# Gate and value halves of a pair's accumulator, and a new order for the first part, in a fused attention and MLP kernel

## The chip, the cores and the metric

The kernel runs on one core of one Trainium2 chip. The metric is the time of one execution on the device, in microseconds (us). Engines are called by their short names in the profile: PE is TensorE (PEld its weight loads), DVE VectorE, ACT ScalarE, POOL GpSimd, and SP the queue that issues most DMAs.

## The reference

The input is a gated linear attention over 4 batches, 8 heads, 768 steps and head size 48, followed by two MLPs over the 3072 tokens.

```
S = 0                                     # complex state, 48 x 48, per batch and head
for t in range(768):
    S = (a_re_n + i a_im_n)[t] * S + k[t] v[t]^T      # a normalised to |a| <= 0.999
    y[t] = q[t] @ S_re
x   = y as 3072 tokens x 384
xn  = x / sqrt(mean(x*x) + 1e-6) * rms_g
x2  = (silu(xn @ w_gate) * (xn @ w_val)) @ w_out      # w_gate, w_val: 384 x 1536
h   = x2 @ w_in                                       # 384 x 2048
out = (h * clip(h + 3, 0, 6) / 6) @ w_out2
```

All inputs arrive in 32 bit floats or, for the weights, as 64 bit words that the kernel turns into 32 bit floats itself. Each large product is made of three matmuls with 32 bit operands split into a high and a low part (`mm3`, lines 735 to 737).

## The kernel before

The time axis is cut into seven units (32 steps twice over at the ends, 64 in between; `UNITS`). A unit goes through these steps, each a small function that issues a few instructions:

- The recurrence of the decay (`steps_norm`, `steps_scan`): 16 or 32 steps of a multiplication (L442) and an addition that reads it (L446) on VectorE, then the scaled keys and queries `X2` and `P`, which also go to memory (L499) and come back as `K` (L536).
- The attention products (`steps_G`): transposes to `psT` (L597), which ScalarE copies to `XTt` (L603); the scores `psS` (L650); the sums `psU` of K and V (L667, L668), from which VectorE makes the new state `Sst` (L638); the outputs `psY` (L678, L687), which ScalarE and GpSimd normalise into `Yt` (L695 to L703); and the transposes to `psX` (L712), split into the halves `xh` and `xl` (L717, L719).
- The first MLP's gate and value products (`steps_M`), for 256 tokens at a time. 12 column blocks j are taken in pairs. One pair has one accumulator tile `pm` in PSUM, 128 partitions of 1024 floats, with two tiles in flight. It holds four quarters of 256: gate and value of the even and of the odd j. Each quarter takes 9 matmuls (three k, three of `mm3`), a tile 36. Then ScalarE applies the Silu to the two gate quarters into `sg` (L756), VectorE multiplies by the two value quarters (L758), and the result goes to memory (L760). There are 12 such passes and 72 tiles.
- In between, weights are loaded and split (L301 to L328) for the first MLP, and then for the rest (`decode`).

All of this, up to about 640 us, is the first part. What sets its order is a long string, `ORDER`: each two characters are the number of a step in the list `steps`, and each time that a number comes up the step issues its next piece. The order of instructions on each engine follows this string, and an engine executes its own in order; semaphores that the framework places keep data right between engines. Behind it follow the second product of the first MLP (`po`, with `uu` read back from memory) and the second MLP (`ph`, `po`), whose order comes from `run` and is not touched.

What the change touches is the tile `pm` in `steps_M` (lines 743 to 767) and the string `ORDER`.

Of the kernel before, what the change touches and what calls it, by code (L numbers as in the profile page):

```python
# [30 lines left out]

DIGITS = "0123456789abcdefghijklmnopqrstuvwxyzABCDEFGHIJKLMNOPQRSTUVWXYZ+-"
ORDER = (
    "000F00010R0R1f0R020R0R0R0R0R020G0R0S0S030S03040S0506080S070b0S0S0b0c0c0S0d0S0H0d120e0T0e0K0T0a0f0T0f0g0T0g0h0h0T090I0i0T0i0j0k0k0T0L0T0J0l0l0m0j0m0n0n0T0o0o0p0U"
    "0p0j0u0q0q0v0r0U0r0v0s0U0t0U0w0t0U0x0U0t0y0z0U1f0U0A170U0A0V11170B0D150V0C1g0V15181h0V0V0V0V0E0V0V11130W0W1h110W181i0W140Q0W110W2r1i0W0W1j0W161k0X2t161a2u1l111b"
    "1n0X1m1z1a2v1z192z1A191A0X1B2s2x2z1B1e1b3b1C2F2y2K0X1C2z1e1D2z1o1d2w1d1D0X1c2A0X2A1E1c2K0OkH2A1E1p2A1F1F0X0X2C1G2B1G2C1H0M1H2D2H0N2K1I1p0X2D1I1q1J1q2G0Y1J0Y1K2D"
    "1r1K1s1L0Y2D2H1L2E2L0Y1v1M2L2L1t2L2M1M2G1N2H1y1N2J0Y2P0Y1u1O2I2P1O2K1Q1Q2N2P1R0Y1R1P2N2N0Y1P1S2N0Y1S0P0Z2O2I2Q1T2I2Q1T2Q1U0Z1U4D1V4J1w0Z1P1V4Q271W4W284E4X1x4F1W"
    "4K280Z4L4P4Y4R2S4S4G4M1X4T4Z0Z0Z4+4U1X4V0Z504-1Z291Y4H2g0Z4N1Z501+2Z511+gj2Z1-570Z581-1Y0Y20202b212+4O0Z4I2+1Y5253210+2V220+220+230+4m2d2V230+242e592425502e5a4P"
    "262f0+2W2a26540+265e2h2c5k2i3b2R5f2j5b0+555l0+2k2W565m2X4l5n5d2R5c0-2X5o5g2-5p2k2R2l2n2m2-5d2R2Y5h5r4p5x4t0-2o2Y305s5t4p3c5i5u2R5y0-304p2T324t0-0-5d2R2R5j374n0-"
    "5v2U32314p5q4o3d4r5q3d4q375q5E5z4t0-314t5A3e5w5F394v4s395B4u0-4v0-344v3410364v10363535383e5C3f103a5D4w3a4w4w105G4w333g103h5H3j104x1010383i3v4P5I5J5K4z104z4z5R3v"  # L40
    "5L5M5R3w334B5N4z3w5O5D5P4A3x5S5T7z5R3x3y3y5S5S5Q4y3z4C3z6a5Q5Z5+3A5U5U3k636g3A6b5-6c6d606e3l3B5U616h3B3C3C5Q5D643D3D5U3E65623l6i6j663E4y3F6k676f6m3F3m693G686l69"
    "3G6m5V5V6A3H693m3n6n3H6B6t6o6u6G3o5V3I3p6m6H6v6w6C3I4C3J3J3K3K3q6p3r6x0W3L6q5V3M6y0R6r3M5W6I3N6D3N6J3O6E3O6s6z6K3P6z6L6z3P6F6M3Q5X3L6M5X7b6+3L3s3Q6-743R3R7b3S43"
    "6N3S703T6T6U3T752q6V6O3V445X6W763V7b773t715X785Y7c446P3W6Q45793U3W726X6M7a3X6Z7c6R6S736Y4c7c3X7a6Z3u3Y3Y7m7l7l3Z9c3Z9d3+8-9i463+3-9e3U9j953-906Z40963U409k479f41"
    "497e42977m9192424a7z4e8J9l9893999m9a424a9g944b7h7i9b7a4f9n4d9h8K9b4g7h4g7d4h7i7n7d9o4j9o7d9p7n9v9b9w9x9q9y7d9r9z489C7d9A4i4k7A9s9I9D7j9E7B7f8R7d9B9F7d9t9G8N7B8R"
    "9J9u7j9o9H8N9B9K9L9M7k7k7C7o8N8L7o7p7C7q9P8N7g9Q9O7D9N8O7p9V7E7q7F8R7v7r7r8P7v7u8M7x9R9O7Ga07H9Wa1a28T7I9B9S8T7x9Ta67J8Ra39X9Y7u7T8S8T7y7T8T7s7U7U7J8U8U7K7Va47V"
    "7W9-7W7X8Ua77X8U8Va5a89U7s8Q7Y7Y7K9Z7Z7y9+8X7Z8X7+7+9-7-8X7t7L7t7-807wa97w9O808Xaaab8Z8Yad7MaeafbX81adae81ad82ae9-8Wayacac7N82alaraEagasatam7P8383au84agazan84ag"
    "aFaGaxacaoaHav85apaA85aBawag8WaqaI86aJ7O86aC88aDah8+ah88aKaxaY87aK87b289ah898a8a8bahaLaM7SaZaR8baN8c8ca+8daOaP878+8db38e7Q8r8eaSaQaT8saxb4aUa-aVb00+8f8f8gaW8hb5"
    "b18hai0Tb68s8i8gb7aXbzajajaK8t8ibzbzaXbJb8b88j8jbKbmd6b9ajbfbabb8kbn8A8k8l8lbg7Rbobsaj8ub8bJ8gbh8m8x8y8makbAbpbc8nbiaXbj8n8obdbtbkbA8obubXd5bv8p8q8y8zblbqbebAbr"
    "bybB8vbBblbwbxbydNdTdOdPdQ8qbydnbl8qbKbB8B8C8Ddt8EdUdV8E8wdodp8FdudvbLbBdqdrdsdR8HdwbL8Gddd9dz8IdxdZdydWdzbBdSdXdYbGdAbYbCbGdGbDbZdHdZbBdBdIdddCd+bEd9d9bFbBbHbZ"
    "d7b+dDd9dzd-e4e0dae5e1dJdEbHb+e2dMbFdZdKdLe3b-e6dFbIc0c3dMbMc1bIdbdfddbMbOc4bObNead8c2bPe7eoc5e8dddfcfbPc5e9epdebUbUeacfebeqdfcgbNdfeubVcgchc6bVbSchbSdgcidgcicj"  # L50
    "cjeackbWckdgbQbWdMerevdgc6ehcleiclcmc7cmcnecejcnewc8dhdjcobQdjcecobRcpbTdjbRc9cpcbexcqescccqdjdceydkeddlcrekcreecsbTen0ScsctcteCeAcueBelefemeBeCcaegeBcueteCezeE"
    "cweAeDdmencwdieWeJcxcvePcxcyf0eKeEencyeLeQczeReXeMeSczcveVcAf1eTeYeEdieAcAeUeNeOcveZeEcBe+cPeFcdcBeFeVeFf2cCcCf3cDfkflfmcDcEf4eFdmf5eGcFe-eHcQeHf6cFfqcQfrfsftcG"
    "cGfnf6eHeHf7cHeIfdeVcHfecIfof8cIf6cEfufpf+fwcRcJcJffcKcKfXcLcEcLf9fvcScYfjcMfwfgcMfhfafbficTfcfxfjcNfXfycOfzcOfDfKfAfEfBcVfYfQcWfXfFcOc+fGc-fRfZd0fYd0fjfLd1fHfC"
    "fJfIfMfwfZfYcWfNgjfShufJfZfTfUhYg6fVi20-cXcUfOfZfWfPg6d3hZ0Ui3h+cZi4gkfWhth-hBi5fZfZimi6fJgli7d4hBi0ini1i8isioi8d2itf-iuivipfWhLgliqgmhxfZhxg4gmgng4g3g3hvg5g7iw"
    "hRhxg7irhxhSg5g0ixgohyg1hzg2gpiyg1g2grg8hBgsiygqhMhBhNiyhThDi9g8ifhOhUiahwhXhPgag9hDgthDg9gthCgagbgDgDgdhQgEhDhVgbgEigihgdibgugFgFhWiihXgegGgugcgcgvgGgHhEhEgfhA"
    "gei8gggHicgwidijgIizikiFiGieiAgIgJiHgxgJilgfhEhEhFiBgygKgKgggLgLhHilgzhHgMiliLiMiSgMiChHgNgNiTiZgOhXhJgOgPiUiVgPiIgQiJgQiDiZgRgRhHhIiEi+gSgSgUgUiNiZiOiKiWgVgViX"
    "gWiPj0i+iQiRiLghi+iYgWgii-gXiYgXjijjjoj0gYgTjkgYgZjljmj5gZiLjng+jbj6g+jpj0g-gTjcj0ghgijd10g-hGh1j7hGjqh1h2jrjsjej8gTh0iYjfh2j9jghbjtgBjhh3h3jah4j1gCj1hKjujhjujI"
    "jujvh4h5jwjOjxjPh5h6jygAj1h6jJh7jQh0jRh7h0jKhcjSh8j1jzh8h9jBjLhc0XhdjCjMjTjAjDjEhfhKjNj2kjhhjFhahiklhajHjhjGkHj3hmjUjUjHj3k6hakcjVjWhikdk7klhnhgklj-kehokjkljUk8"
    "k9j3kihkk0kflkhjkghollklkjhlk1j3hphrloj4kkkkk2jXklkakhkIjHjYkkklkbk3k5jZhek4j+kikulokrkmk5lPlokulChslDlIkrhqlsk5lEkJlQlFlRkJkKlskKlGlVlWlSlJkilKknkpktlmkplLlolX"
    "lTlYkLlZlHlUlOlMlNlOktl+l-kvlslnkqkokvlql-kMkskPkqlpkNkwksmdlrmjlum0lsm1mkmem6mfkwmlm7mglukOkxkykQlukxltkykSkRkAkzlulvkSkTkAkTkUlvkUkVkVkBkzkDmhmilvkWkWkXkXmmmn"  # L60
    "kYkYlvq6kDkZkZm8k-mom2m3m4m9l-mpmak-lwlyl0l0kBlOk+kFl1kCkFmpmclylyl1mDk+mQm5mQ2pmbmcmQmJmEl2l2mKmFlyl3lAmql3lzl4mwl4l5mxk+mRmRmRmTmLkCl5mrmGmHmMmsmpmNl6mymzmImO"
    "l6mAmPkEmPkGmSl7mtkGn9ocl9l8nanbnfl8mumBnglanhmPmvlanclbmCockEndl8mCmTldnemcmYnimTnjlelxnklxn2nlmZm+nlmToclflfn3lgn4nmnsntmClim-nulcmUlBq4mUocq4nnnonvn5npmUnwq5"
    "n6q4ocnln7n0nymUljmVq4nqocnrn1lhlBq5q4nxocogq5q7oimWq4nymWoiq4n8ohogojmWn8mWq5ojoenzq6nZq6odq6nAq5n+oqq8n-nyq5oaq6oaq6nFo3o4o0q5q7o5o1o6oamXoro7o2ohq6nGq8q7o9ou"
    "n8q9obobo8nBnCnHnIosoboko9ouq7ouolnJq7nMolnNnDofnEqanLq7q7nSounTnUq8nKnOovnPoko9nVnWoyowotnLonq8oyomoyoyq8q8nQoAonq8oVqaoAomoWo-nYqbnLp0p1oxp2oXnRqanXoAozooopoA"
    "oBoBnYoIq9p5oOoPoJq9q9oooKnYq9qaqaoYoQoZo+qcoLq9qaqdoRoMoBp3opq9p4oUoSoBp5oNoCoToEqaqboEqboEqcoDoHqbpjoUp6pppcqcp7qcpqp8qcoEqbpkqcpdpeqboFprplp9pfpsqbpgpaqdoGqd"
    "p5phqdqcqdptpupZpmqeoHpvqdpnpbpZqeoUqepZoDpipop+pvp+pipWpvqfpXpJpwp+p+pxpWpypPpCqeqepDpzpEp-pKpXpQpLq0q0pipApBq0qdpMqfpFq0pGpNpRqfqfpXpHpSpVqfpTpOpWq1pUqeq3q2pY"
    "qfpVq3qfq2pIpI0VpIpZqepVq2q3"
)
# [1051 lines left out]
```

## Time and profile before

| | us |
|---|---|
| Median of 3 runs | 1206.21 (1202.79 to 1368.59) |
| Profiled execution | 1208.78 |
| Its span, from the first to the last instruction | 1207.0 |
| TensorE busy | 1089.3 (90%) |
| VectorE busy | 779.7 (65%) |
| ScalarE busy | 544.1 (45%) |
| Mean granted clock of TensorE | 0.974 |

The busy time of an engine is the time in which it had at least one instruction; matmuls overlap, so their durations add up to more. Idle time of an engine is put down to what ended it: the line and tile behind an arrow is the work whose end let the instruction go. The granted clock is a share of 2.4 GHz.

### The profile page before, as it was taken

To read this page: it belongs to the slowest core of one execution; us is meant where nothing else is said; L and a number is where in the kernel's file an instruction comes from. 1 tells how busy PE (TensorE), PEld (TensorE's weight loads), DVE (VectorE), ACT (ScalarE), POOL (GpSimd) and SP (SyncE) were. 2 spreads that over 40 slices of the span, in tenths; PEclk is the share of its full clock that TensorE was granted. 3 is DMA by queue.
4 is the path that set the end of the run, shared out by engine and by line. 5 is a ranking of instruction groups with operands and counts; after the bars stand their busy time and mean duration, and the time that the engine had idled before them with its cause. 6 is when DMAs were issued, how large, how long until landed. Compare 5 with 4: busy or idle time off the path is not lost.

```text
span 1207.0 us, 24591 instructions
## 1 busy us (share of the span) xinstructions
PE 1089.3 (90%) x10264; PEld 944.4 (78%) x10264; DVE 779.7 (65%) x1501; ACT 544.1 (45%) x930; POOL 72.8 (6%) x99
## 2 busy tenths in 40 slices
...
GB/s 252 143 173 140 130 46 237 132 88 231 102 107 184 78 98 206 112 118 153 144 177 302 283 191 101 52 44 1 64 68 1 62 70 1 57 31 1 27 1 29
DMA packets 81433, 133.71 MB, mean 111 GB/s; under 512 B 32225, under 2 KB 50786, under 8 KB 80674
## 3 DMA queue, kind: packets, MB, share of 16 engines
...
q10 hardware_dynamic: 656, 0.11, 0.1%
HBM read 89.77 MB, written 34.60 MB: 103 GB/s over the span
## 4 chain that ended last, share of the span: by engine, by line
PE 42%; DVE 5%; DMA 4%; issue 1%; ACT 1%; DVEq 0%; SPq 0%; ACTq 0%
PE po L736 8%; PE po L737 8%; PE po L735 8%; PE ph L735 5%; PE ph L736 5%; PE ph L737 5%; DMA rawc<-in_wgv_dram 3%; PE pm L735 1%; PE pm L736 1%; PE pm L737 1%; DVE wmin L311 1%; DVE words L303 1%; DMA ok_dr<-okc 1%; DVE ul L906 1%; DVE words L301 0%
## 5 line engine op out<-in xcount | busy, mean ns | idle before, releaser
L735 PE MATMUL pm<-xh,wg 128*128 128x256 f32 x864 | 262.3, 304 | 26.6 <-ACT sg L756 20.6
L736 PE MATMUL pm<-xl,wg 128*128 128x256 f32 x864 | 250.3, 290 | 1.5 <-DVE xl L719 1.5
L737 PE MATMUL pm<-xh,wg 128*128 128x256 f32 x864 | 249.6, 289 | 0.0
L735 PEld LDWEIGHTS pm<-xh,wg 128*128 128x128 f32 x864 | 170.4, 197 | 38.1 <-ACT sg L756 25.6
L736 PEld LDWEIGHTS pm<-xl,wg 128*128 128x128 f32 x864 | 170.8, 198 | 1.8 <-DVE xl L719 1.7
L737 PEld LDWEIGHTS pm<-xh,wg 128*128 128x128 f32 x864 | 170.6, 197 | 0.0
L950 DVE SCALAR_TENSOR_TENSOR r<-r,ph 128x512 f32<-128x512 f32 x96 | 65.9, 686 | 104.0 <-ACT r L949 103.8
L952 DVE TENSOR_TENSOR gl<-r,gh 128x512 fp32r<-128x512 f32 x96 | 68.0, 709 | 94.8 <-ACT gh L951 94.5
L736 PE MATMUL po<-gl,w_h 128*128 128x512 f32 x288 | 114.3, 397 | 4.0 <-DVE gl L952 4.0
L949 ACT ACTIVATE r<-ph,biasz 128x512 f32<-128x512 f32 x96 | 65.9, 687 | 112.7 <-PE ph L737 112.5
L737 PE MATMUL po<-gh,w_l 128*128 128x512 f32 x288 | 114.3, 397 | 0.0
L735 PE MATMUL ph<-x2b,wi_h 128*128 128x512 f32 x288 | 113.8, 396 | 0.4 <-DVE r L950 0.4
L736 PE MATMUL ph<-x2b,wi_h 128*128 128x512 f32 x288 | 113.6, 394 | 0.1
L737 PE MATMUL ph<-x2b,wi_l 128*128 128x512 f32 x288 | 113.6, 395 | 0.0
L951 ACT ACTIVATE gh<-r 128x512 fp32r<-128x512 f32 x96 | 60.7, 633 | 114.1 <-PE po L737 87.1
L735 PE MATMUL po<-gh,w_h 128*128 128x512 f32 x288 | 107.1, 396 | 0.0
L906 DVE TENSOR_TENSOR ul<-uu,uh 128x512 fp32r<-128x512 f32 x72 | 52.1, 725 | 71.6 <-ACT uh L905 71.6
L736 PE MATMUL po<-ul,wo 128*128 128x512 f32 x216 | 85.9, 398 | 3.2 <-DVE ul L906 3.1
L905 ACT ACTIVATE uh<-uu 128x512 fp32r<-128x512 f32 x72 | 45.4, 630 | 94.8 <-PE po L737 77.7
L756 ACT ACTIVATE sg<-pm 128x512 f32<-128x512 f32 x72 | 42.4, 597 | 99.1 <-PE pm L737 78.7
L737 PE MATMUL po<-uh,wo 128*128 128x512 f32 x216 | 84.9, 393 | 0.0
L758 DVE TENSOR_TENSOR sg<-sg,pm 128x512 f32<-128x512 f32 x72 | 48.7, 683 | 47.3 <-ACT sg L756 15.6
(130 smaller groups left out, 1999.4 us busy)
## 6 DMA issues: line engine op xcount, KB each, us to landing
...
```

The lines of the kernel that those rows point to most:

```text
L303: nc.vector.scalar_tensor_tensor(out=A, in0=lo, scalar=29, in1=A, op0=ALU.logical_shift_right, op1=ALU.bitwise_or)
L735: nc.tensor.matmul(ps, lhsT=wh, rhs=xh, start=first, stop=False)
L736: nc.tensor.matmul(ps, lhsT=wh, rhs=xl, start=False, stop=False)
L737: nc.tensor.matmul(ps, lhsT=wl, rhs=xh, start=False, stop=last)
L756: nc.scalar.activation(sg, pm[:, :, 0], AF.Silu)
L758: tt(out=sg, in0=sg, in1=pm[:, :, 1], op=ALU.mult)
L905: nc.scalar.activation(uh, uu, AF.Copy)
L906: (nc.gpsimd if n < 0 else nc.vector).tensor_tensor(out=ul, in0=uu, in1=uh.bitcast(F32), op=ALU.subtract)
L949: nc.scalar.activation(r, ph, AF.Relu, bias=biasz[:, 2:3], scale=sixth)
L950: stt(out=r, in0=r, scalar=1.0, in1=ph, op0=ALU.min, op1=ALU.mult)
L951: nc.scalar.activation(gh, r, AF.Copy)
L952: tt(out=gl, in0=r, in1=gh.bitcast(F32), op=ALU.subtract)
```

## The change

The tile `pm` is indexed by half first and by j second, so that the two gate quarters are one piece of 512 floats, and the two value quarters another. In the list of steps the gemms of a pair now stand half by half: both gates, then both values. The string `ORDER` is another one throughout; of its 38 lines the first is shown.

```diff
-    "000F00010R0R1f0R020R0R0R0R0R020G0R0S0S030S03040S0506080S070b0S0S0b0c0c0S0d0S0H0d120e0T0e0K0T0a0f0T0f0g0T0g0h0h0T090I0i0T0i0j0k0k0T0L0T0J0l0l0m0j0m0n0n0T0o0o0p0U"
+    "0F0R0R0000010G0R0R020R0R0R0R0J0R020S0S03030S0405060L080S070S0H0I0b0b0c0c0c090d0d0N0S0e0e0f0f0g0g0S0S0h0h0S0i0i0T0k0K0k0l0j0j0l0T0j0m0T0m0a1f0u0n0n0T0o0T0o0p0T0T0p"
...
-            mm3(hold[j // 2][:, j % 2, w], wh[:, k, w], wl[:, k, w], xh[:, k], xl[:, k], k == 0, k == KT - 1)
+            mm3(hold[j // 2][:, w, j % 2], wh[:, k, w], wl[:, k, w], xh[:, k], xl[:, k], k == 0, k == KT - 1)
...
-            nc.scalar.activation(sg, pm[:, :, 0], AF.Silu)
+            nc.scalar.activation(sg, pm[:, 0], AF.Silu)
             yield
-            tt(out=sg, in0=sg, in1=pm[:, :, 1], op=ALU.mult)
+            tt(out=sg, in0=sg, in1=pm[:, 1], op=ALU.mult)
...
-        for j in range(J1):
+        for i in range(J1 // 2):
             for w in range(2):
-                for k in range(KT):
-                    out.append((("gemm", h, j, w, k), lambda j=j, w=w, k=k: gemm(j, w, k)))
-            if j % 2:
-                out.append((("silu", h, j), lambda j=j: silu(j)))
+                for j in (2 * i, 2 * i + 1):
+                    for k in range(KT):
+                        out.append((("gemm", h, j, w, k), lambda j=j, w=w, k=k: gemm(j, w, k)))
+            out.append((("silu", h, 2 * i + 1), lambda i=i: silu(2 * i + 1)))
```

The number of instructions of each kind and shape is the same on every engine. Three places of the order:

On PE, in the fourth unit's first pass of `steps_M`, the tile `pm_4675`, the 34th of the 72, before (a name's number tells buffers apart; `[waits ...]` names the engine whose semaphore the instruction waits for, where it does):

```order
L735 MATMUL pm_4675<-xh_4345,wg_313 128x256
L736 MATMUL pm_4675<-xl_4346,wg_313 128x256
L737 MATMUL pm_4675<-xh_4345,wg_313 128x256
L735 MATMUL pm_4586<-xh_4345,wg_763 128x256 [waits Activation_49]
L736 MATMUL pm_4586<-xl_4346,wg_763 128x256
L737 MATMUL pm_4586<-xh_4345,wg_763 128x256
L735 MATMUL pm_4675<-xh_4345,wg_342 128x256 [waits Activation_49]
L736 MATMUL pm_4675<-xl_4346,wg_342 128x256
L737 MATMUL pm_4675<-xh_4345,wg_342 128x256
L735 MATMUL pm_4675<-xh_4345,wg_342 128x256
```

The same tile of the change, there `pm_4607`:

```order
L735 MATMUL pm_4607<-xh_4308,wg_396 128x256
L736 MATMUL pm_4607<-xl_4309,wg_396 128x256
L737 MATMUL pm_4607<-xh_4308,wg_396 128x256
L735 MATMUL pm_4607<-xh_4308,wg_396 128x256 [waits Activation_49]
L736 MATMUL pm_4607<-xl_4309,wg_396 128x256
L737 MATMUL pm_4607<-xh_4308,wg_396 128x256
L735 MATMUL pm_4765<-xh_4308,wg_924 128x256 [waits DVE_49]
```

Before, the mark stands behind the tile's 18th matmul, since its Silu was issued there; in the change it stands behind the 33rd, with three left. The first matmul into a further tile waits for VectorE's multiplication out of an older one, in both.

On DVE, at the start of the first unit's recurrence, before:

```order
L442 TENSOR_TENSOR m4_158<-LAt_110,P_100 128x192
L328 SCALAR_TENSOR_TENSOR wg_151<-wdA_108,gcol_66,wg_151 128x256
L446 TENSOR_TENSOR P_100<-m4_158 128x2x48
L442 TENSOR_TENSOR m4_163<-LAt_110,P_100 128x192
L446 TENSOR_TENSOR P_100<-m4_163 128x2x48
L442 TENSOR_TENSOR m4_167<-LAt_110,P_100 128x192
L328 SCALAR_TENSOR_TENSOR wg_151<-wdA_108,gcol_66,wg_151 128x256
L446 TENSOR_TENSOR P_100<-m4_167 128x2x48
```

and in the change:

```order
L442 TENSOR_TENSOR m4_164<-LAt_110,P_100 128x192
L446 TENSOR_TENSOR P_100<-m4_164 128x2x48
L442 TENSOR_TENSOR m4_167<-LAt_110,P_100 128x192
L446 TENSOR_TENSOR P_100<-m4_167 128x2x48
L442 TENSOR_TENSOR m4_172<-LAt_110,P_100 128x192
L446 TENSOR_TENSOR P_100<-m4_172 128x2x48
```

The pieces of the weight split that stood between a multiplication and its addition come later here, so the pairs stand back to back.

On SP, the loads of the start, before (V is the values of the first unit, S its keys and queries, `wraw` raw weights):

```order
L316 DMA wraw_170<-in_wgv_dram 128x1536
L526 DMA V_173<-in_v0_dram 64x1536
L316 DMA wraw_179<-in_wgv_dram 128x1536
L431 DMA S00_182<-in_s_all_dram 128x768
L431 DMA S01_197<-in_s_all_dram 128x768
L316 DMA wraw_199<-in_wgv_dram 128x1536
L316 DMA wraw_210<-in_wgv_dram 128x1536
L316 DMA wraw_213<-in_wgv_dram 128x1536
L345 DMA LAt_110<-in_a_all_dram 128x3072
```

and in the change:

```order
L316 DMA wraw_162<-in_wgv_dram 128x1536
L431 DMA S01_170<-in_s_all_dram 128x768
L316 DMA wraw_175<-in_wgv_dram 128x1536
L316 DMA wraw_199<-in_wgv_dram 128x1536
L431 DMA S00_214<-in_s_all_dram 128x768
L316 DMA wraw_257<-in_wgv_dram 128x1536
L345 DMA LAt_110<-in_a_all_dram 128x3072
L526 DMA V_260<-in_v0_dram 64x1536
L316 DMA wraw_326<-in_wgv_dram 128x1536
```

The load of V moves behind the second load of `LAt`, and more weights are fetched ahead of it.

## Rows read from the trace of the kernel before

**Rows 1.** The page's totals: busy us (share of the span) and instructions by engine.
```profile
PE 1089.3 (90%) x10264; PEld 944.4 (78%) x10264; DVE 779.7 (65%) x1501; ACT 544.1 (45%) x930; POOL 72.8 (6%) x99
```

**Rows 2.** Stretches: length, busy us (instructions) PE PEld DVE ACT POOL, clock, DMA, GB/s.
```profile
40.00:280.00 240.00, 204.58 (x3093) 188.40 (x3092) 217.50 (x459) 149.97 (x267) 11.50 (x24) 0.96 0.47 143
280.00:636.00 356.00, 326.75 (x4789) 309.42 (x4790) 270.20 (x551) 179.90 (x318) 25.29 (x40) 0.95 0.49 138
636.00:1207.00 571.00, 556.13 (x2374) 445.18 (x2372) 258.46 (x416) 196.88 (x317) 26.55 (x25) 0.99 0.24 72
```

**Rows 3.** Waits of PE, 280 to 636 us: us in total, times, longest.
```profile
PE pm L735 <- ACT sg L756: 15.8, 16, 3.7
PE psU L667 <- DMA K<-k_dr: 4.7, 5, 3.0
PE psY L678 <- ACT Yt L703: 2.5, 1, 2.5
...
PE pm L735 <- DVE sg L758: 1.0, 3, 0.3
```

**Rows 4.** Waits of PE, 40 to 280 us.
```profile
PE pm L735 <- ACT sg L756: 4.8, 4, 2.2
```

**Rows 5.** Timeline of PE: start, us, instruction [idle before <- what ended it].
```profile
360.81 0.58 PE L735 MATMUL pm<-xh,wg 128*128 128x256 f32 x1 [3.68 <-ACT sg L756]
...
371.74 0.28 PE L737 MATMUL pm<-xh,wg 128*128 128x256 f32 x1
372.71 0.38 PE L735 MATMUL pm<-xh,wg 128*128 128x256 f32 x1 [0.69 <-ACT sg L756]
```

**Rows 6.** Timeline of ACT around the same two places.
```profile
358.86 1.28 ACT L756 ACT_TABLE_LOAD   x1
360.16 0.60 ACT L756 ACTIVATE sg<-pm 128x512 f32<-128x512 f32 x1
...
372.06 0.60 ACT L756 ACTIVATE sg<-pm 128x512 f32<-128x512 f32 x1 [1.45 <-PE pm L737]
```

**Rows 7.** Groups of instructions, whole span: count | busy us, mean ns | idle before.
```profile
L949 ACT ACTIVATE r<-ph,biasz 128x512 f32<-128x512 f32 x96 | 65.9, 687 | 112.7 <-PE ph L737 112.5
...
L758 DVE TENSOR_TENSOR sg<-sg,pm 128x512 f32<-128x512 f32 x72 | 48.7, 683 | 47.3 <-ACT sg L756 15.6 <-PE pm L737 13.5 <-issue 6.8
...
L756 ACT ACTIVATE sg<-pm 128x512 f32<-128x512 f32 x72 | 42.4, 597 | 99.1 <-PE pm L737 78.7 <-DMA u_dr<-sg 15.3 <-DVE m L442 4.9
```

**Rows 8.** Half-clock stretches: one, sums over three and over six; last, full clock.
```profile
359.40:366.20 6.80, 5.39 (x25) 5.39 (x26) 1.94 (x4) 4.57 (x8) 0.00 (x0) 0.50 0.02 8
...
sum 13.40, PE 11.99 PEld 11.03 DVE 5.93 ACT 6.13 POOL 0.00; mean PE 4.00 PEld 3.68 DVE 1.98 ACT 2.04 POOL 0.00
...
sum 33.50, PE 31.09 PEld 30.06 DVE 21.29 ACT 13.97 POOL 0.79; mean PE 5.18 PEld 5.01 DVE 3.55 ACT 2.33 POOL 0.13
...
367.00:387.00 20.00, 17.92 (x150) 16.66 (x148) 13.31 (x34) 9.76 (x17) 0.00 (x0) 1.00 0.89 263
```

**Rows 9.** Timeline of DVE in the first unit's recurrence.
```profile
22.20 0.36 DVE L442 TENSOR_TENSOR m<-LAt,P 128x192 f32<-128x192 f32 x1
22.47 0.55 DVE L301 TENSOR_SCALAR wdA<-wraw 128x768 int32<-128x768 int32 x1
...
25.40 0.36 DVE L442 TENSOR_TENSOR m<-LAt,P 128x192 f32<-128x192 f32 x1
25.79 0.26 DVE L446 TENSOR_TENSOR P<-m 128x96 f32<-128x96 f32 x1
```

**Rows 10.** Timeline of SP: DMAs issued at the start.
```profile
34.87 0.33 SPq L345 DMA_DIRECT2D LAt<-in_a_all_dram  x1
...
48.32 1.80 SPq L536 DMA_DIRECT2D K<-k_dr  x4
```

**Rows 11.** Waits of DVE, 40 to 280 us.
```profile
DVE sg L758 <- ACT sg L756: 2.4, 2, 1.3
DVE sg L758 <- PE pm L737: 2.3, 2, 2.0
```

More of the change, by code (lines that the diff above doesn't have):

```diff
@@ L67 @@
-    "qfpVq3qfq2pIpI0VpIpZqepVq2q3"
+    "0F0R0R0000010G0R0R020R0R0R0R0J0R020S0S03030S0405060L080S070S0H0I0b0b0c0c090d0d0N0S0e0e0f0f0g0g0S0S0h0h0S0i0i0T0k0K0k0l0j0j0l0T0j0m0T0m0a1f0u0n0n0T0o0T0o0p0T0T0p"
+    "0T0q0v0q0v0r0T0r0s0U110w0t0U0t0x0y0M1f120t17170U0z150A0U150U0U0A0B0U0U1811180U0V0D160V1g0V0O0C1h160V110V0V0V0V1a1h0V1a0E0W110W1i0W1i190W19111j130W2r2t1k1l1n1b0W"
+    "1b0W1c1m140W1z0W1z2v2u2x0X1A2z3b1d1A0X2s1B1c2z1o1B2z1C2y1p1C1D2z1e1p1D0X2A2F2A1E2w0X2K1d1E1F2K1F0X2A1e2q1G2C2A2B1q1G2D1H2H1q2K1H2D1r1I0X2D1I2C1J2D1J2G0X0Q2E1K0X"
@@ new lines @@
+    "2L1s1K2L0X2L2H1L1t1L2G1M0Y2L2I1M1N0Y1u1N0Y2M1O1v2I1O1x2J0Y2I1Q1P0Y1Q2K2P1R0Y2N1R1P1S0Y1w0Y1S0Y1T2P2N0Z1T1U1P2N2H1U2N2P2O1V2Q271V0Z2Q1W2Q1W1X281X0Z2S4Q1Y0Z4l1y1Z"
+    "1Y1Z4m4W284R1+1+4X4Y4Z291-0Z4D4+2g4E0P1Y1-2b4F4J4S202+4K4L4-4T2d4U204G0Z4V4M2W0Z2150212W504N0Z51222e222c2+232e4H234I52530Z240+4O244P574P0+252R5e4P262R2R2f5f265g"
+    "542R262R0+2i582j2Z0+2R5k2k0+0+595l2R552k5h5a502-565m5d5b2-5c2V0+2l2n2h3b2a2Z0+305i2V5n4t2X5j5o305d5p2m2Y4p2o5r2T5x3c0+5q4p2X5s0-5t2Y313d0-312U32335u4n0-3d5y0-4p"
@@ new lines @@
+    "4t4p335z380-4r5A5q5E325v3e0-4t4q340-340-4t4v5K384v5L5w3e5B0-3a394o5d4v4u3910355C5M3a4v5D105q354w4w3f4w103g36104w104x375F5G36105N3h4z4z3j5R4s5H103i3v3v3w103w4z10"
+    "5R3x4z5R3x5O4B5I3y375D4A5J5P5S3y5Q5S3z3k5T5S4y3z6a5Q3A5Z6b5U6g5+633A6c5U6d5-6h3B3B3l5D643C3C655U0R6e3D605U3D4y3E663l6i6j67613E6f3m6m6k5Q6l3F5V6m3m3F3G3n3G3H4C5V"
+    "4C623H5V5V3o5W6A6B3I3p3I6G686C69696D6H5X5X6n6o6E3J6F6I3J6J6p6m3K3r3K6t3q3M5X3M3N6K3N6q696L7b3O3L6r6u3O6v6w6x3s6M3P3L3L3P6M3Q6+743Q7e6-753R3R6M6s436y3t703S715X76"
@@ new lines @@
+    "5Y3S3T776z78443T6z728K79737b6N3V6T7c3V8J6U7b3W7z446O6V6W6z3WbX6P6X3u3U456Y7a6Q7c6R6S7c7m3X4c3X3U3Y7a7l9c6Z3Y3U9d9i3Z6Z8-3Z9j3+9e3+9f3-3-95407l904940474a91969g97"
+    "9h6Z417h42427m7i4a429k4e9l984b4f927i464g7a939m7z7h999a4d4g949b7j7n4h9n7j9bgj7d484j9o9p9v7d9o7d9q9w7n9r7d7A8R7B9C8R9x4i8N7B4k9I7d9D9b8N7d9s9y9J7f9E9o9t9z9F7C7g9A"
+    "9K9G7d8R9H9u7o7k9B8L8N9L9B7C7D8N9O9M7k9P7E7o9N7q7p8M8P9O7p7q7F8O7r7v7H7Ia09Q9V8T7G8R7Ta6a19W9X9Y9R9Za77J7r9S9T7T7v8Ta28S7U7J7u8T7U7y8T8U7V8U7V7W7u7W7y7X7X7Y7w8U"
```

54 lines of the change are left out of this document (22 added, 32 removed).

## The prediction

> **What bounds the kernel now.** I read the page's totals first [rows 1]: TensorE is busy for 1089.3 of 1207.0 us, so an order can give back only some of 118 us of idle TensorE, and what is lost at a lower clock. The stretches say where that lies [rows 2]. From 636 us on TensorE is busy 556.1 of 571 us, with work that the change does not touch. From 40 to 280 us VectorE is busy 217.5 of 240 us, TensorE 204.6: there the recurrence and the splitting of the weights on VectorE set the pace, and TensorE waits for what they bring. From 280 to 636 us it turns round: VectorE has 270.2 of 356 us, TensorE 326.8. There TensorE's in-order queue sets the pace, with 29.2 us idle, and a stall of it is worth its own length.
>
> Who ended that idle time [rows 3]: by far the largest part is `pm` matmuls that waited for a Silu, 15.8 us in 16 waits. Between 40 and 280 us the same wait is 4.8 us in 4 [rows 4]. Two places show what it is. At 372.02 us, where the last matmul ends, the stream stops for 0.69 us until the Silu that began at 372.06 us on ScalarE has been read out [rows 5, 6]. In front of 360.81 us it stops for 3.68 us: the Silu that it needs stands behind a table load of 1.28 us, and starts at 360.16 us. In the order of the kernel before both are matmuls in the middle of a tile's own 36, marked with a wait on ScalarE. The Silu had been issued as soon as both gate quarters were done, and the next matmul into the same tile then waits until the Silu is through.
>
> **The change, part by part.**
>
> *Layout.* The Silu and the multiplication read 128x512 as before, in one piece now and not in two of 256. The Silu takes 597 ns [rows 7]. Its nearest neighbour that reads one piece of the same size from PSUM is the Relu, 687 ns, which applies a scale and a bias as well, so an end of the price is +0.09 us for each; nothing there excludes a gain of like size. I take 0: each Silu is the same instruction on as many elements, and ScalarE has 179.9 of 356 us [rows 2].
>
> *The marked waits.* Counted over the whole order, 40 of the 72 tiles had their Silu issued ahead of their last matmul, and 38 had a matmul marked to wait for it; now 18 are early and 16 are marked. So the new layout does not take the wait away: where a Silu is early, the program still holds the next matmul, though that one writes the other half. What the change does is to have fewer such tiles, as the gate half is closed late in most: 54 of the 72 Silus now come behind all 36 matmuls. Behind 280 us the marked tiles go from 27 to 12. At the mean price, 15.8 us over 27 marks, 0.59 us each, 15 fewer give 8.8 us. But those that stay are less covered: 5 of the 12 have no matmul between the Silu's last input and the wait (0.69 us each, as in rows 5) and 2 have three of 0.12 us (0.33 us), 4.1 us in all, against 6 and 7, 6.5 us, before. By that share the gain is 15.8 x (1 - 4.1/6.5) = 5.8 us. I take 7. In front of 280 us the 4.8 us give nothing, as VectorE covers them.
>
> *The later Silu.* The multiplication follows it on VectorE and frees the tile for the pair after the next. Silu and multiplication are 0.60 + 0.68 us [rows 7]. In the closest places of the new order 9 matmuls of 0.12 us (150 in 17.92 us busy [rows 8]), 1.1 us, stand between a pair's end and the next use of its buffer, so one such place costs some 0.3 us, which is what the three such waits behind 280 us cost now, 1.0 us [rows 3]. I add 1 us, between 0 and 3.
>
> *The clock.* The granted clock is one half (1.2 of 2.4 GHz) in stretches that begin in or behind long gaps. Three of them, 277.5 to 280.8, 359.4 to 366.2 and 550.6 to 553.9 us, begin at a wait for a Silu, the middle one at that of 3.68 us; around the wait of 0.69 us the clock stays whole, 1.00 from 367 to 387 us [rows 8]. At half clock a `pm` matmul takes 0.22 us of the stream (25 in 5.39 us busy), not 0.12, so of 11.99 us of busy TensorE in the three, 0.45 or 5.4 us is lost. I take half of it, 2.5 us, since some long waits for a Silu will stay.
>
> *VectorE's order in front of 280 us.* A multiplication of the recurrence and the addition that reads it start 0.39 us apart when they stand back to back; with another instruction between, the next one starts after 0.27 us [rows 9]. So a back-to-back pair costs 0.12 us. Up to the 25th tile (281 us) there are 144 pairs of an instruction and its reader before and 138 now, over the whole part 324 and 313. At the start the new order has more (43 against 39 up to the first `pm` matmul), and with them 4.3 us more work of VectorE ahead of that matmul; ahead of the 25th tile it has 3.1 us less. As VectorE paces here, the ends are +4.3 and -3.1 us. I take -1, because the early debt is work that need not be done later.
>
> *Queues that steps are moved past.* On SP the load of V for the first unit moves behind six loads of weights, the two of S and the second one of `LAt`, which left at 34.87 us. The sums that read V need K too, whose loads left at 48.32 us [rows 10]; that is 13 us of cover, so V costs nothing. Without the cover it would be a start of the sums up to 13 us later. On POOL, 72.8 us busy of 1207 [rows 1], only places change.
>
> *TensorE's other waits.* For K and `Yt` behind 280 us they are 4.7 and 2.5 us [rows 3]. Each has a new place that no row shows, so the bounds are 0 and twice the 7.2 us. I take 1 us less: behind 280 us the old order has four loads of K with under 9 us of matmuls between the work that frees the buffer's queue place and the sums that read it, the new one three.
>
> *Sum.* -7 + 1 - 2.5 - 1 - 1 = -10.5 us. The profiled execution took 1208.8 us, its span and 1.8 us around it, 2.6 us above the median of 1206.2 us of the runs shown. Carried to the median: **1196 us**.
>
> **The rivals.**
>
> *Most of the gaps close, and the clock holds (1170 to 1182 us).* An order that is searched as a whole may close gaps of every kind. Behind 280 us there are 29.2 us idle and 31.09 us of busy TensorE at half clock [rows 2, 8], 0.45 of it 14 us. Were two thirds of both gone, the gain would be 29 us, 1177. For it: the marks were more than halved. Against it: the marked places that stay are the uncovered ones, and the chains over K and `Yt` are as long as before. The Trainium skill, "TensorE: Matmul & The Clock Gate", section "A second HAM failure mode: psum-queue depth-cycling", says that short idles of TensorE between groups of matmuls, as buffers in PSUM are cycled, let its clock drop and rise again and again. By that rule the small waits for a Silu would cost clock too, and this rival would be likely; the trace does not bear it out for the 0.69 us one (granted clock 1.00 around it).
>
> *The layout does what its shape suggests (1183 to 1188 us).* If an early Silu held the other half no more, all of the 15.8 and the 5.4 us would go, 21 us: 1185. The marks in the order speak against it. The Trainium skill, "PSUM — Partial Sum Buffer", section "Terms", says that two engines must not be in one bank of PSUM at a time; by that the old Silu, which reads both banks, needs the wait, and the new one does not. No run here shows it.
>
> *Nothing measurable (1202 to 1210 us).* What is taken from the waits for a Silu turns up at K, `Yt` or the multiplication, as all of them end where ScalarE or VectorE is late.
>
> *Slower (1210 to 1230 us, or more).* One mechanism: with the Silu behind the whole pair, the multiplication waits at the head of VectorE's queue in front of 280 us, where VectorE paces, and all that stands behind it is late. Such waits, for the Silu or the matmuls, are now 2.4 us in 2 and 2.3 us in 2 [rows 11], 1.2 us each. 24 tiles fall into that stretch: 28.8 us if each waits, 24 more than now, 1230 us. It decides where less than 1.3 us of VectorE's work stands between a pair's end and its multiplication; ten such tiles, 12 us, take up my gain and more. Against it: in nearly all tiles VectorE's work ahead is within 5 us of what it was.
>
> **How the numbers follow.** Forecast (a gain of 4 to 18 us, 1188 to 1202) 0.48; nothing measurable 0.20; the layout's own gain 0.06; most gaps closed 0.12; slower 0.14, of it 0.05 beyond 1230. The range reaches into both outer cases, 1178 to 1214 us, and leaves out 0.06 below and 0.11 above. About 2% (24 us) is what a measurement of this kernel can tell from no change. Faster by more is under 1182 us, 0.12; slower by more over 1230 us, 0.05; within it 0.83.
>
> **What would show it.** `pm`'s waits for a Silu behind 280 us fall from 15.8 to 7 to 10 us, in about half as many; half-clock time behind 280 us falls by some 10 us; the 25th tile begins about where it did, 281 us. The prediction is wrong if VectorE's waits for a Silu or `pm` in front of 280 us pass 10 us, if the part up to 636 us ends where it did though the marked waits are gone, or if the waits for K or `Yt` double.

## The result, and the profile after

| | before | change |
|---|---|---|
| Median on the same chip, 4 runs each (us) | 1207.82 | 1175.86 (1173.06 to 1176.71) |
| Profiled execution, span (us) | 1208.78, 1207.0 | 1173.06, 1171.3 |
| TensorE busy (us) | 1089.3 | 1068.4 |
| Mean granted clock | 0.974 | 0.995 |

The ratio is 0.9745, 95% interval 0.9706 to 0.9784: 2.5% faster. It compares fast runs alone, without the one of 1368.59 us among the four of before, which is a slow run. The forecast of 1196 us and its range (1178 to 1214) were missed on the fast side; the time is that of the rival "most of the gaps close, and the clock holds", which had a chance of 0.12.

The page's totals of the change, which answer to [rows 1]: VectorE and ScalarE have the same work as before, TensorE is busy 20.9 us less with the same 10264 matmuls.

```profile
PE 1068.4 (91%) x10264; PEld 927.6 (79%) x10264; DVE 776.8 (66%) x1501; ACT 544.6 (46%) x930; POOL 74.8 (6%) x99
```

Where the time went is seen when both traces are cut at the same work: from the first `pm` matmul to the 25th tile, from there to the last `pm` matmul, and the rest. The stretches of before, in the columns of [rows 2]:

```profile
92.75:281.10 188.35, 175.08 (x2453) 162.74 (x2454) 168.21 (x351) 120.50 (x204) 7.31 (x16) 0.95 0.46 137
281.10:635.50 354.40, 325.15 (x4783) 307.93 (x4782) 270.20 (x551) 178.34 (x315) 24.79 (x40) 0.95 0.49 138
635.50:1207.00 571.50, 556.63 (x2376) 445.58 (x2375) 258.46 (x416) 197.35 (x317) 27.05 (x25) 0.99 0.24 72
```

and of the change:

```profile
93.70:269.10 175.40, 167.56 (x2452) 156.87 (x2452) 163.94 (x347) 117.71 (x199) 8.10 (x16) 1.00 0.52 150
269.10:599.70 330.60, 311.78 (x4783) 296.92 (x4782) 269.41 (x550) 180.38 (x318) 24.06 (x40) 0.99 0.52 150
599.70:1171.30 571.60, 556.08 (x2377) 445.66 (x2375) 258.19 (x416) 197.04 (x317) 26.91 (x25) 1.00 0.24 72
```

The change starts 0.95 us later, gains 13.0 us up to the 25th tile and 23.8 us behind it, and nothing in the rest. The first two rows hold the same matmuls, so a difference in busy TensorE is the clock. It is 7.5 us in the first row and 13.4 in the second, 20.9 together; idle TensorE (length less busy) falls from 13.3 to 7.8 us and from 29.3 to 18.8 us, 15.9 together. So more than half of the gain between these two executions is clock. The profiled one had the highest mean clock of the change's four (0.995, the others 0.988 to 0.992); 13 later runs of before had 0.972 to 0.983, so the difference is not one of the two executions alone.

The half-clock stretches say the same. Before, nine of them lie between the first and the last `pm` matmul; their sum:

```profile
sum 54.80, PE 50.21 PEld 46.80 DVE 37.97 ACT 26.58 POOL 1.58; mean PE 5.58 PEld 5.20 DVE 4.22 ACT 2.95 POOL 0.18
```

In the change there are two:

```profile
374.10:377.50 3.40, 3.40 (x53) 3.31 (x46) 1.69 (x3) 1.08 (x2) 0.00 (x0) 0.50 0.03 6
445.80:449.20 3.40, 3.40 (x16) 3.40 (x17) 3.37 (x5) 3.32 (x4) 0.00 (x0) 0.50 0.79 175
```

43.4 us less of TensorE busy at half clock, times the 0.45 of the prediction, is 19.5 us, near the 20.9 measured. Not all of that is shorter stops: the change's two longest, 2.58 us at 276 and 2.68 us at 574 us, had no half clock in or behind them, while all six of 2 us and more in before had.

The waits of TensorE behind the 25th tile in the change (269.1 to 599.7 us), to be held against [rows 3]:

```profile
PE pm L735 <- ACT sg L756: 9.3, 8, 2.6
PE pm L735 <- DVE sg L758: 5.4, 4, 2.7
PE psU L667 <- DVE Sst L638: 1.7, 1, 1.7
PE psX L712 <- ACT XTt L603: 1.2, 1, 1.2
```

The waits for a Silu fall from 15.8 to 9.3 us, those for K (4.7 us) and `Yt` (2.5 us) are gone, those for the multiplication rise from 1.0 to 5.4 us.

### The profile page after: what moved, and what is told of

It reads as the page before. It is cut to its first block, busy times and chain, and to the rows that moved or that the text cites. A ratio compares the mean times of both kernels' runs of the same rounds, so it can differ in the third digit from the quotient of the medians.

```text
span 1171.3 us, 24602 instructions
## 1 busy us (share of the span) xinstructions
PE 1068.4 (91%) x10264; PEld 927.6 (79%) x10264; DVE 776.8 (66%) x1501; ACT 544.6 (46%) x930; POOL 74.8 (6%) x99
## 4 chain that ended last, share of the span: by engine, by line
PE 65%; DVE 13%; issue 8%; DMA 6%; ACT 5%; POOL 1%; SPq 0%; DVEq 0%; ACTq 0%; POOLq 0%
PE po L737 8%; PE po L736 8%; PE po L735 8%; PE pm L735 6%; PE pm L736 5%; PE pm L737 5%; PE ph L735 5%; PE ph L736 5%; PE ph L737 5%; DMA rawc<-in_wgv_dram 3%; PE psT L597 3%; PE psY L687 2%; PE psS L650 1%; ACT sg L756 1%; DVE X L354 1%
## 5 line engine op out<-in xcount | busy, mean ns | idle before, releaser
L735 PE MATMUL pm<-xh,wg 128*128 128x256 f32 x864 | 256.4, 297 | 19.3 <-ACT sg L756 11.6
L736 PE MATMUL pm<-xl,wg 128*128 128x256 f32 x864 | 245.4, 284 | 0.5 <-DVE xl L719 0.5
L737 PE MATMUL pm<-xh,wg 128*128 128x256 f32 x864 | 244.9, 283 | 0.0
L735 PEld LDWEIGHTS pm<-xh,wg 128*128 128x128 f32 x864 | 165.3, 191 | 28.3 <-ACT sg L756 14.1
L736 PEld LDWEIGHTS pm<-xl,wg 128*128 128x128 f32 x864 | 165.6, 192 | 0.8 <-DVE xl L719 0.8
L737 PEld LDWEIGHTS pm<-xh,wg 128*128 128x128 f32 x864 | 165.4, 191 | 0.1
L442 DVE TENSOR_TENSOR m<-LAt,P 128x192 f32<-128x192 f32 x192 | 68.0, 354 | 4.0 <-ACT LAt L412 0.2
```

Source lines behind the costliest of these rows:

```text
L442: tt(out=m4, in0=la, in1=pj, op=ALU.mult)
```

## Experiments

**Is it the layout?** The old layout and the old list of gemms take the new string almost as it is: one Silu moves behind its gates, and the gemms of one tile are refilled, since their weights come later than the string assumes.

```diff
 # the kernel before, with the change's order
-ORDER = (before)
+ORDER = (change; silu of one tile of the unit 4 behind its second gate; last tile of the unit 0 refilled)
```

> The old layout of the accumulator (and the old list of gemms) with the order of the change. Theory 'order': the whole gain of 32 us lies in the order, the layout is worth nothing: 1172 to 1180 us, half-clock time and idle TensorE as in the change. Theory 'layout': the halves in one piece shorten the Silu's hold on the next matmul; then part of the gain goes, 1185 us or more, and the waits of pm for a Silu in the first part rise from 14 us by 5 us or more.

Measured: 1181.68 us (ratio to before 0.9824, 0.9779 to 0.9868), between the two ranges expected, so the time alone does not decide. A Silu takes 598 ns, 597 in the change, a multiplication 680 in both, and the waits of `pm` for a Silu are 11.9 us in 12, 11.6 in 11 in the change. The last thing to look at is one stretch of 40 tiles in which both orders are the same but for the one Silu, from the 29th tile to the 69th. In the change:

```profile
301.90:582.50 280.60, 266.22 (x4166) 252.90 (x4165) 226.23 (x472) 151.30 (x269) 18.17 (x34) 0.99 0.49 141
```

and with the old layout:

```profile
308.10:588.80 280.70, 266.88 (x4166) 252.96 (x4165) 226.02 (x471) 151.29 (x269) 18.05 (x34) 0.99 0.49 141
```

0.1 us in 280. The 6 us lie ahead of it: a stop of 1.67 us for weights at the refilled tile, and a half-clock stretch of 6.8 us at 278 us. The reverse experiment, the new layout with that same order, settles what was left:

```diff
 # the change, with the order of the experiment above
-ORDER = (change)
+ORDER = (that of the old-layout kernel; three gemms of the refilled tile later still)
```

> The new layout with the very order of the old-layout experiment (three gemms of one tile later by a few places, since their weights are not ready). Theory 'the layout is worth nothing': within 4 us of its 1181.7 us, and 281 us from the 29th to the 69th tile as in both. Rival 'layout': 1176 us or less.

1184.18 us (0.9851, 0.9794 to 0.9907), against 1181.68: the layout alone is worth nothing that can be measured. From the 29th to the 69th tile it takes 282.8 us, with 10.2 us of half clock in place of the 6.8 us that the old layout had there.

**Is it the marked waits?** In the order of before, only the 40 early Silus are moved, each behind the last gemm of its tile. For one tile (j 4 and 5 of the unit 3):

```diff
 gemm j 7, value, k 2
-silu j 4, 5: Silu on ScalarE
 ...
 gemm j 4, value, k 2
+silu j 4, 5: Silu on ScalarE
 gemm j 8, gate, k 0
 silu j 4, 5: multiplication on VectorE
```

> The order of before, with each of its 40 early Silus moved behind the last matmul of its tile and nothing else moved. Theory 'marked waits': the 20.6 us of pm waiting for a Silu go almost wholly, and with them the half-clock stretches that begin at such waits (277, 359, 550 us): 1180 to 1192 us. Rival 'handed on': each later Silu makes the multiplication and with it the next use of the buffer late, pm waits for VectorE by 10 us or more: 1200 to 1215 us.

Measured: 1209.05 us, ratio 1.002 (0.9993 to 1.0046). The rival is right. The waits for a Silu, 20.6 us in the first part of before, are gone, and this stands at the head of TensorE's waits from the first to the last `pm` matmul:

```profile
PE pm L735 <- DVE sg L758: 18.8, 14, 3.9
```

It was 5.6 us in 5. How a wait is handed on is seen at the largest new one, on ScalarE:

```profile
314.20 0.94 ACT L391 ACTIVATE T<-T,biasz 128x768 f32<-128x768 f32 x1
315.17 0.84 ACT L392 ACTIVATE T<-T 128x768 f32<-128x768 f32 x1
315.92 0.19 ACT L392 ACTIVATION_READ_ACCUMULATOR T<-T 128x1 f32 x1
316.12 1.28 ACT L756 ACT_TABLE_LOAD   x1
317.42 0.60 ACT L756 ACTIVATE sg<-pm 128x512 f32<-128x512 f32 x1
```

on VectorE and on TensorE:

```profile
318.05 0.69 DVE L758 TENSOR_TENSOR sg<-sg,pm 128x512 f32<-128x512 f32 x1 [4.61 <-ACT sg L756]
```

```profile
318.79 0.55 PE L735 MATMUL pm<-xh,wg 128*128 128x256 f32 x1 [3.87 <-DVE sg L758]
```

The late Silu falls behind the normalisation of the next unit (L391, L392) and a table load; VectorE waits 4.61 us for it, and TensorE 3.87 us for VectorE. So the number of marks is not what made the change faster. That they still cost something shows in the other direction, with the change's Silus moved ahead:

```diff
 gemm (last gate of the tile)
+silu: Silu on ScalarE
 ...
 gemm (last of the tile, or some behind)
-silu: Silu on ScalarE
```

> The change, with each Silu issued as soon as its gates are done: 49 of the tiles have it ahead of their last matmul, against 18. Theory 'marked waits' at 0.59 us for a mark: 31 more marks cost 18 us and some 5 us of clock, 1190 to 1200 us, pm's waits for a Silu over 25 us in the first part. Rival 'the marks are covered in this order': within 5 us of 1176 us.

1219.21 us (1.0116, 1.0091 to 1.0141), 43 us more than the change and beyond either expectation:

```profile
PE pm L735 <- ACT sg L756: 36.0, 31, 4.5
```

That is 24 us more of these waits than in the change (11.6 us in 11); the rest is clock, 44 us at one half between the first and the last `pm` matmul. So a late Silu pays in the new order and did not in the order of before. That ScalarE and VectorE are free in the new one when a tile ends is argued from the place above, and not shown for all tiles. The complement is to take the change's own 18 early Silus and move them as above:

> The change with its 18 early Silus moved behind the last matmul of their tile: no tile is marked in its middle. Theory 'each mark costs': pm's waits for a Silu (11.7 us in the first part) go, 1164 to 1170 us. Rival 'handed on', as with the order of before: the waits come back as waits for the multiplication, 1173 to 1182 us.

1167.25 us (0.9711, 0.9665 to 0.9757): 8 us below the change by the medians, 4 us by the ratios, each to its own runs of before. The two intervals overlap, so a gain over the change is likely and not shown. No `pm` matmul waits for a Silu any more; those for the multiplication are 9.5 us in 10, 7.2 in 8 in the change.

**Is it the stretch in front of 280 us, or the one behind?** The prediction gave the first nothing. Two hybrids, in the old layout, change orders at the 25th tile:

```diff
-ORDER = (before)
+ORDER = (change up to the first gemm of the 25th tile) + (what is left, in the order of before)
```

> The old layout; the order of the change up to the first matmul of the 25th tile, and from there what is left in the order of before. Theory 'both stretches count': the 12 us that the change gains up to the 25th tile stay, 1192 to 1198 us, and the 25th tile begins at 269 to 273 us. Rival 'VectorE paces the front', as the prediction had it: what is gained there is work of VectorE put off, and the rest gives it back, 1202 to 1210 us.

```diff
-ORDER = (before)
+ORDER = (before up to the first gemm of the 25th tile) + (what is left, in the order of the change)
```

> The other way round: the order of before up to the 25th tile, then what is left in the order of the change. Theory 'both stretches count': the 24 us behind the 25th tile stay, 1181 to 1187 us, with under 15 us of half clock behind it. Rival 'an order fits only its own start': at the seam and behind it new stops of 2 us and more, 1192 us or more.

Measured: 1195.75 us (0.9921, 0.9888 to 0.9954) and 1184.07 us (0.9853, 0.9803 to 0.9902). Against the 1204.6 us of before beside them that is -9 and -21 us: both stretches count, and what is gained in front is not paid back behind. How much the front is worth is not shown. The -21 us of the second one are nearly what the old layout gained with the whole new order (-24), so the two parts do not simply add. And in the profiled execution of the first one the 25th tile begins at 277.2 us, not at 269 to 273 as expected, with 17.1 us of half clock ahead of it; its two stretches, to be held against the first two of before, are

```profile
93.60:277.20 183.60, 174.37 (x2453) 162.99 (x2453) 164.48 (x346) 117.91 (x199) 7.34 (x16) 0.95 0.50 143
277.20:626.97 349.77, 324.00 (x4782) 307.04 (x4782) 270.29 (x551) 179.76 (x318) 24.75 (x40) 0.96 0.49 142
```

That is 4.8 us less than before in front and 4.6 us less behind, where the order is that of before. The second hybrid, with the order of before in front, took 183.43 us there: by so much, mostly clock, two executions of one order differ. The medians above are surer than these rows.

The first hybrid shows besides how loosely a stop and the clock hang together. It and the old-layout kernel issue the same instructions up to the 25th tile, and both stop for 1.67 us at the refilled tile, at 138 and 139 us. The 17 us behind that in the hybrid:

```profile
140.10:157.20 17.10, 17.10 (x224) 15.93 (x217) 11.09 (x21) 8.63 (x18) 1.50 (x4) 0.50 0.08 21
```

and in the old-layout kernel:

```profile
139.00:156.00 17.00, 15.92 (x376) 14.48 (x377) 15.05 (x30) 12.62 (x25) 2.10 (x4) 1.00 0.25 66
```

The same stop, once with 17.1 us of half clock behind it, in which TensorE is busy without a break, once with none.

**Is it the transfer out of `sg`?** In before the Silu waits 15.3 us in 5 for the transfer of an older `sg` [rows 7]; in the change 3.9 us in 2.

```diff
-            sg = mo.tile([128, 2, 256], F32, name="sg", tag="sg")
+            sg = mo.tile([128, 2, 256], F32, name="sg", tag="sg", bufs=3)
```

> The kernel before with three buffers for sg in place of two, order and layout untouched. In the trace of before the Silu waits 15.3 us in 5 for the transfer of an older sg to memory. Theory 'the long stops behind Silus come from the transfer': the stops at 277 and 550 us (2.2 and 2.7 us) and their half-clock stretches go, 1198 to 1202 us. Rival 'ScalarE would be late anyway': within 3 us of before.

1205.77 us, ratio 1.0008 (0.9977 to 1.0038). The waits for the transfer fall to 1.5 us, the stop at 277 us shrinks to 1.42 us and the one at 550 us goes, but seven stops of 1.5 us and more stay, for K, `Yt` and others (eight before). One cause of long stops taken away moves nothing that can be measured.

**What does a stop cost in clock?** A kernel of bare matmuls with stops of known length:

```diff
+        for rep in range(3):
+            for m in LADDER:                 # 1, 2, 3, 4, 5, 6, 8, 10, 12: m + 1 copies on ScalarE
+                gap(pm, m)                   # the next matmul reads what the last one writes
+                pm = burst(252 + 9 * rep)    # matmuls 128x256 without a stop
+        for m in (1, 2, 3):
+            for _ in range(8):
+                gap(pm, m)
+                pm = burst(36)
```

> Nothing of the reference is computed: long runs of pm's matmuls, 128x256, with a stop of known length between them, made by 2 to 13 operations of ScalarE that the next matmul waits for, each length three times; then three trains of eight stops with 36 matmuls between. Theory 'long stops only': behind stops of up to about 1 us the granted clock stays whole, behind those of 2 us and more a half-clock stretch of 3.4 to 6.9 us follows, each worth 1.6 to 3 us beside the stop itself. Rival 'any stop': the trains of short stops lower the clock as well, which would make each wait of 0.6 us cost more than its length. Third: length does not decide, the same stop lowers the clock in one of its three places and not in another.

Three of its stops in the timeline of TensorE (start, us, instruction, and in brackets the idle time before it):

```profile
163.77 0.39 PE L109 MATMUL pm<-xl,wg 128*128 128x256 f32 x1 [1.68 <-ACT xl L117]
...
196.23 0.39 PE L109 MATMUL pm<-xl,wg 128*128 128x256 f32 x1 [1.97 <-ACT xl L117]
...
500.87 0.39 PE L109 MATMUL pm<-xl,wg 128*128 128x256 f32 x1 [1.97 <-ACT xl L117]
```

and the stretches behind those three, and behind the stops of 3.41 us at 300 and 3.98 us at 335 us; the last is the train of eight stops of 0.82 us:

```profile
163.80:170.60 6.80, 6.80 (x57) 6.80 (x58) 0.00 (x0) 0.00 (x0) 0.00 (x0) 1.00 0.00 0
196.50:199.90 3.40, 3.40 (x18) 3.40 (x18) 0.00 (x0) 0.00 (x0) 0.00 (x0) 0.50 0.00 0
500.90:507.70 6.80, 6.80 (x57) 6.80 (x58) 0.00 (x0) 0.00 (x0) 0.00 (x0) 1.00 0.00 0
...
300.40:307.20 6.80, 6.74 (x56) 6.74 (x57) 0.00 (x0) 0.01 (x1) 0.00 (x0) 1.00 0.00 0
333.00:339.80 6.80, 4.86 (x22) 4.86 (x23) 0.00 (x0) 1.70 (x7) 0.00 (x0) 0.50 0.00 0
998.00:1045.00 47.00, 40.43 (x322) 38.81 (x321) 0.00 (x0) 5.12 (x16) 0.00 (x0) 1.00 0.00 1
```

| stop (us) | places | with half clock in or behind it |
|---|---|---|
| 0.8 to 1.7 | 12 | 0 |
| 0.8, 1.1, 1.4 in trains | 24 | 0 |
| 2.0 | 3 | 2 |
| 2.3 | 3 | 2 |
| 2.8 | 3 | 3 |
| 3.4 | 3 | 2 |
| 4.0 | 3 | 3 |

In this kernel the first and the third theory hold together: short stops cost their length and nothing more, even in trains; of stops of 2 us and more, 12 of 15 had 3.4 or 6.8 us at half clock that began in them or behind them. Which of them did not is not told by their length.

**The same in the kernel.** From the kernel with all Silus late, five long stops are put in, or twenty short ones:

```diff
+REPEAT = {(2, 1, 5): 5, (3, 1, 5): 5, (5, 0, 1): 5, (5, 0, 5): 5, (5, 1, 1): 5}
...
-            nc.scalar.activation(sg, pm[:, 0], AF.Silu)
+            for _ in range(REPEAT.get((u, h, j // 2), 1)):
+                nc.scalar.activation(sg, pm[:, 0], AF.Silu)
```

and in the order the Silu of these five tiles right behind their gates. For the short stops `REPEAT` is empty, and the Silus of twenty tiles stand behind their gates.

> The change with all Silus late (1167 us), and five tiles far from each other whose Silu stands again in front of the value half and is computed five times over, so that the next matmul waits for the last one: five stops of some 3 us, 15 us in all. Theory 'long stops lower the clock': 15 us of idle TensorE and half-clock stretches of 3.4 to 6.8 us behind most of the five, 8 to 15 us more: 1188 to 1197 us. Rival 'a stop costs its length': 1177 to 1184 us.

> The same base, with twenty tiles whose Silu stands again in front of the value half, computed once: twenty stops of some 0.7 us, 14 us in all. Theory 'long stops lower the clock': idle TensorE as in the kernel with five long stops, but no more half-clock time than the base (7 us) or one stretch more: 1177 to 1184 us. Rival 'any stop lowers it': over 20 us of half clock, 1188 us or more.

Measured: 1191.06 us (0.9878, 0.9811 to 0.9945) and 1175.2 us (0.977, 0.9715 to 0.9825), against 1167.25 (0.9711) without them; the second is just below its expected range. A kernel that differs from the one without them by two moves, the last one below, ran beside these two and took 1164.34 us. From the first to the last `pm` matmul, in the kernel with all Silus late:

```profile
92.74:593.12 500.38, 478.30 (x7233) 453.45 (x7234) 433.84 (x897) 297.05 (x516) 32.24 (x56) 0.99 0.52 152
```

with five long stops:

```profile
92.71:621.80 529.09, 495.81 (x7233) 470.09 (x7234) 434.07 (x897) 309.11 (x536) 31.62 (x56) 0.95 0.50 144
```

with twenty short ones:

```profile
92.71:604.07 511.36, 483.42 (x7233) 456.35 (x7234) 433.81 (x897) 297.32 (x516) 32.05 (x56) 0.98 0.51 148
```

The long stops add 11.2 us of idle TensorE and 17.5 us of busy TensorE for the same 7233 matmuls. Three of them stop a `pm` matmul for 3.20 us each and have 3.4, 13.6 and 3.4 us of half clock behind them. The other two repeated Silus keep ScalarE from other steps: `psY` waits 3.32 us at 312 us and `psT` 1.42 us at 558 us, and the clock is at one half there as well:

```profile
311.50:321.70 10.20, 9.44 (x101) 9.13 (x102) 4.31 (x12) 4.07 (x9) 0.74 (x2) 0.50 0.20 56
557.30:567.50 10.20, 9.97 (x102) 9.38 (x103) 5.64 (x11) 3.11 (x8) 0.72 (x2) 0.50 0.24 75
```

The short ones came to less than planned, 5.9 us idle and 5.1 us busy; of their three half-clock stretches one lies at 121 us, ahead of all of them, and two at stops of 2.2 and 1.9 us (557 and 576 us). From 130 to 555 us, where 11 waits for a Silu add up to 7.8 us and none is over 1.3 us, the clock is whole:

```profile
130.00:555.00 425.00, 405.05 (x6438) 382.31 (x6436) 364.06 (x753) 257.83 (x440) 22.61 (x44) 1.00 0.50 141
```

So the long stops put into this kernel cost more in clock than in waiting, and the short ones from 130 to 555 us did not lower it. Length alone does not tell, though: the stretch at 121 us, 6.8 us at half clock, follows stops of 0.80 and 0.89 us, which had none behind them in the kernel with all Silus late, and the stop of 1.42 us above had 10.2 us.

**A better version.** In the kernel with all Silus late the longest stop left is 2.64 us at 566 us, for a multiplication behind pieces of weight decoding.

```diff
 silu j 8, 9 and j 10, 11 of the unit 5: Silu on ScalarE
+silu j 8, 9 and j 10, 11 of the unit 5: multiplication on VectorE
 ... pieces of the decoding
-silu j 8, 9 and j 10, 11 of the unit 5: multiplication on VectorE
```

> The change with all Silus late, and the multiplications of the last two tiles before the last unit issued right behind their Silus, ahead of four pieces of weight decoding on VectorE: the stop of 2.6 us at 566 us should shrink to about 1 us and its half-clock stretch go: 1163 to 1167 us. Rival 'the decoding comes late instead': no gain against 1167 us.

1164.34 us (0.9684, 0.9626 to 0.9743): 3.2% below before by the ratio, and all its runs (1162.85 to 1168.26 us) lie below those of the change, though the intervals of the two ratios overlap; it is not to be told from the 1167.25 us without the move. The time is in the expected range, but not for the reason given: the stop only went to 2.12 us, as most of the decoding was issued ahead of the Silu as well, and 3.4 us of half clock stayed at it.

Eight of these kernels side by side, from the first to the last `pm` matmul (idle is length less busy; half clock is the sum of the stretches in it). A row is one profiled execution. Up to the 25th tile the order of before had 20.5 us of half clock in its own and 10.2 us in that of "old, then new"; differences of that size between rows say little:

| us | length | idle | busy | half clock |
|---|---|---|---|---|
| before | 542.8 | 42.5 | 500.2 | 54.6 |
| change | 506.0 | 26.7 | 479.4 | 6.8 |
| old layout, new order | 511.4 | 29.0 | 482.4 | 13.7 |
| order of before, Silus late | 542.1 | 40.9 | 501.2 | 58.0 |
| change, Silus early | 550.4 | 51.5 | 498.9 | 44.4 |
| new, then old | 533.4 | 35.0 | 498.4 | 47.8 |
| old, then new | 513.2 | 30.6 | 482.6 | 13.7 |
| change, all Silus late | 500.4 | 22.1 | 478.3 | 6.8 |

Busy TensorE is some 476 us and 0.45 of the half-clock time in all of them, within 3 us.

## Why the prediction was wrong, point by point

*The clock* is the step that failed: -2.5 us in the sum, -20.9 measured. The price of a stretch was right (0.45 of the busy time in it). Wrong was which stretches were counted: only the three that begin at a wait for a Silu, and half of them. The six others, 41 us of half clock at stops for K, `Yt`, `FTp`, `Sst`, `xl` or a multiplication, were taken as given, though the term on TensorE's other waits supposed that such waits move. The pieces were all in the text of the first rival (29.2 us of gaps, 14 us of clock); it was put at 0.12, because the marks that stay were the uncovered ones. The experiment with the order of before shows that marks were the wrong thing to count. That rival's time came in part by luck: it had two thirds of the idle time behind 280 us go, and one third went (29.3 to 18.8 us), while nearly all of the clock's loss there went; and it counted nothing in front, which gave 12 us between the two profiles.

*In front of 280 us* the sum had -1 us, and 4.8 us of waits for a Silu were said to be covered by VectorE. It was -13.0 us to the 25th tile, +0.95 at the start; the hybrid with the new order only there is 9 us faster than before by its median, the surer number. VectorE was busy 168.2 of 188.35 us in that stretch: 89% busy is not a floor. This is the second failed step, and in part the first again, as 7.5 of the 13 us are clock.

*The layout* at 0: right, shown in both directions.

*The marked waits* at -7 behind 280 us: 15.8 became 9.3 us, -6.5. Right in size, and no cause by itself: in the order of before the same waits, all taken away, come back as waits for the multiplication.

*The later Silu* at +1, bounds 0 and 3: +4.4 us behind the 25th tile, outside; but from the first to the last `pm` matmul these waits are 5.6 us before and 7.2 now, +1.6.

*TensorE's other waits* at -1, bounds 0 and twice 7.2 us: K and `Yt` went wholly, -7.2 us. The count of loads with little cover, four to three, told nothing of it.

With the two above, idle TensorE behind the 25th tile fell by 10.4 us where the sum had -7.

*SP and POOL* at 0: no wait for V appears, right.

*The slower rival*, multiplications that wait at the head of VectorE's queue in front of 280 us: such waits for a Silu or `pm` up to the 25th tile were 4.7 us in 4 [rows 11] and are 2.1 in 4. It is refuted there. Its mechanism is what kept the order of before from gaining with late Silus, behind 280 us.

*Short idles and the clock.* The rule of the Trainium skill, "TensorE: Matmul & The Clock Gate", section "A second HAM failure mode: psum-queue depth-cycling", was set aside in the prediction because of one wait of 0.69 us. The bare kernel agrees with setting it aside: none of 36 stops of 0.8 to 1.7 us lowered the clock. In the full kernel it is open, with half clock behind stops of 0.89, 1.16 and 1.42 us. The mistake lay not there but in leaving the half-clock stretches of the long stops for K, `Yt` and others where they were.

Of what was to be seen, the waits for a Silu behind 280 us came out as said (9.3 us, 7 to 10 forecast); the half-clock time behind 280 us fell by 27 us (33.5 us [rows 8] to 6.8) and not by some 10, and the 25th tile begins at 269.1 and not at 281 us. None of the three signs of being wrong came: they looked for a gain that stays out, and none for one that is larger.

What stays open: which property of the new order makes its stops fewer and shorter. Two single causes were taken out of the order of before, the early Silus and the transfer out of `sg`, and neither moved the time. Why one stop lowers the clock and another of the same length does not is open too.
